# A sparse attention and Fourier mixing kernel: x added by GpSimd for six output items, a new item order, and U two items behind V

## The chip, the cores and the metric

The kernel runs on one core of a Trainium2 chip. The core has a matrix engine (TensorE, PE in the profile), a vector engine (VectorE, DVE), a scalar engine (ScalarE, ACT), GpSimd (POOL) and SyncE (SP), which work through their own instruction queues and wait for each other by semaphores. Matrix products land in PSUM, eight banks of 128 x 512 float32; everything else lies in SBUF. Sixteen DMA engines move data between SBUF and the device memory. The metric is the device time of one execution in microseconds; the median of three runs before the change is 427.61 us (427.32 to 427.89).

## The reference

The first half is causal attention on 8 batches and 8 heads, 576 positions, head size 64. Four heads see a local window of 32, four see the positions of the same residue modulo 32. Its output, x (8 x 576 x 512), goes through a Fourier mixing layer of 64 modes and a channel matrix:

```python
X = np.fft.rfft(x, axis=1)
Xr, Xi = (np.real(X[:, :n_modes]), np.imag(X[:, :n_modes]))
Yr = np.einsum('bmd,mde->bme', Xr, w_r) - np.einsum('bmd,mde->bme', Xi, w_i)
Yi = np.einsum('bmd,mde->bme', Xr, w_i) + np.einsum('bmd,mde->bme', Xi, w_r)
Y[:, :n_modes] = Yr + 1j * Yi
y = np.fft.irfft(Y, n=S, axis=1)
u = x + y
return (u + np.maximum(u @ w_ch, 0.0)).astype(np.float32)
```

So each output row is U + relu(V) with U = x + y and V = U @ w_ch. The output is 9.44 MB of float32.

## The kernel before

Three stages are interleaved by hand; the order of each engine's instructions is the order of the program text. The attention runs batch by batch. Beside it and after it the 64 modes' complex weights stream in (128 matrices' halves through GpSimd's DMA queue, 81 MB with the attention's inputs), and each mode is multiplied with the spectra of all 8 batches. In the meantime x @ w_ch and x itself are prepared in float16 (`v0s`, `xos`, and for the last 64 positions of each batch `v0h`, `xoh`), and as modes get ready, `renew` (L948) adds the contribution of three quarters of the modes to them. What is left for the end is the contribution of the last 16 modes.

The end, which the change is about, starts after the last mode (L1042). The output is cut into 18 items (L973 to L977). Items 0 to 15 are a pair of batches (2P, 2P+1) and one of four sets of 128 rows, t = 0 to 3; sets t and t+1 (t even) are the even and odd rows of the same 256. Items 16 and 17 are the last 64 rows of four batches each. The order before is, for P0 in (0, 2): t = 0 to 3 outside, P = P0, P0+1 inside, so neighbouring items are of different pairs of batches.

Every item k goes through these steps:

- `v_early(k)`, L984 to L987: two identity matmuls on TensorE copy the prepared x @ w_ch into a PSUM pair from pool `p` (three pairs of banks). `u_early(k)`, L989 to L992: two identity matmuls copy the prepared x into a PSUM pair, from pool `p` for even k and from pool `u` (one pair) for odd k.
- `new_rows`, L994 to L1003: for each batch of the item one matmul of 32 rows adds the last modes' part, from `zzs` to V and from `yys` to U. The 32 rows of batch b are those of the row group b modulo 4 of the TensorE array.
- `v_done(k)`, L1008 to L1013: ScalarE writes relu(V) to `rl` in SBUF, float32; four such tiles rotate.
- `u_done(k)`, L1015 to L1033: VectorE adds U from PSUM and `rl` to the output tile `osb` (five buffers, shared with the weights), and SP issues the output DMA, 512 KB. Item 0 goes in two halves. The last two items go as eight DMAs of 128 KB, from SP and ScalarE in turn.

After a prologue for items 0 and 1, the loop at L1065 runs U one item behind V: passes of V of k, passes of U of k-1, rows of V of k, rows of U of k-1, relu of k, addition and DMA of k-1. Before item 8 a held spectrum for batches 4 to 7 is made (L1066 to L1069), in a buffer of pool `p`. GpSimd does nothing in this stage; its last instruction is the last weight DMA (L190).

Of the kernel before, what the change touches and what calls it, by code (L numbers as in the profile page):

```python
# [12 lines left out]
AluOp = mybir.AluOpType  # L13
# [43 lines left out]
def kernel(  # L57
# [10 lines left out]
    nc = tc.nc  # L68
# [9 lines left out]
    def psum_pools(**bufs):  # L78
        pctx.close()
        pss.clear()  # L80
        for n, c in bufs.items():
            pss[n] = pctx.enter_context(
                tc.tile_pool(name="ps_" + n, bufs=c, space=PSUM)
            )

    def psum(kind, half=False, pair=False):
        if pair:
            return pss[kind].tile([128, 2, 512], FP, tag=kind, name=kind)
        if half:
            return pss[kind].tile([128, 1024], F16, tag=kind, name=kind)  # L90
        return pss[kind].tile([128, 512], FP, tag=kind, name=kind)
# [158 lines left out]
    def act_copy(out, in_):  # L250
        nc.scalar.activation(out=out, in_=in_, func=ACTF.Copy)  # L251
# [445 lines left out]
    def out_cols(t):  # L697
        if t < 4:
            return ds(256 * (t % 2) + 128 * (t // 2), 128)
        return ds(512, 64)  # L700

    v0s, xos = {}, {}
# [30 lines left out]
    def spec_z(g, bq, zp):  # L733
        for e in range(4):
            lhs = YS["YT"][:, e, g, ds(8 * bq, 8), :].rearrange("p x m -> p (x m)")
            nc.tensor.matmul(
                zp, lhs, w_chs["n"][:, e, :], start=(e == 0), stop=(e == 3)
            )
# [129 lines left out]
    xoh = [ptr.tile([128, DM], F16, name=f"xoh{i}") for i in range(4)]  # L868
    zzs = [ptr.tile([128, DM], F16, name=f"zz{i}") for i in range(B)]
    yys = [ptr.tile([128, DM], F16, name=f"yy{i}") for i in range(B)]  # L870
# [31 lines left out]
    A3 = cs["cFl"].rearrange("p a t m -> p (a t m)")[:, 0:S]  # L902
# [64 lines left out]
    for n, i in enumerate([3, 5, 7] + list(range(8, 21))):  # L967
        b, t = n // 2, n % 2 * 2
# [3 lines left out]

    items = []  # L973
    for P0 in (0, 2):
        items += [((2 * P, 2 * P + 1), t) for t in range(4) for P in (P0, P0 + 1)]
    items += [(range(b, b + 4), 4) for b in (0, 4)]
    LAST = len(items) - 1  # L977
    vps, ups, rls, osbs = {}, {}, {}, {}

    def own(item, kept, half):  # L980
        bs, t = item
        return [kept[b][:, t] for b in bs] if t < 4 else [half[b // 2] for b in bs[::2]]

    def v_early(k):  # L984
        vps[k] = psum("p", pair=True)
        for j, r in enumerate(own(items[k], v0s, v0h)):
            nc.tensor.matmul(vps[k][:, j], idn, r, start=True, stop=False)  # L987

    def u_early(k):  # L989
        ups[k] = psum(("p", "u")[k % 2], pair=True)  # L990
        for j, r in enumerate(own(items[k], xos, xoh)):
            nc.tensor.matmul(ups[k][:, j], idn, r, start=True, stop=False)  # L992

    def new_rows(k, acc, spectra):  # L994
        bs, t = items[k]
        for j, b in enumerate(bs):
            q = ds(32 * (b % 4), 32)
            o, cols = acc[:, j % 2], out_cols(t)
            if t == 4:
                o = acc[ds(64 * (b % 2), 64), j // 2]  # L1000
            nc.tensor.matmul(  # L1001
                o, A3[q, cols], spectra[b // 4][q], start=False, stop=True
            )  # L1003

    def pieces(k):
        return [slice(0, 1), slice(1, 2)] if k == 0 else [slice(0, 2)]

    def v_done(k):  # L1008
        rl = ptr.tile([128, 2, 576], FP, tag=("xT", "rl")[k // 2 % 2], bufs=2, name="rl")
        rls[k] = rl[:, :, 0:DM]  # L1010
        vp = vps.pop(k)
        for j in pieces(k):
            nc.scalar.activation(out=rls[k][:, j], in_=vp[:, j], func=ACTF.Relu)  # L1013

    def u_done(k):  # L1015
        bs, t = items[k]
        up, rl = ups.pop(k), rls.pop(k)
        osb = pw.tile([128, 2, DM], FP, tag="w", name="osb")
        for j in pieces(k):
            nc.vector.tensor_tensor(  # L1020
                out=osb[:, j], in0=up[:, j], in1=rl[:, j], op=AluOp.add
            )
            if t < 4:
                rows = out[:, ds(128 * (t - t % 2), 256), :].rearrange(
                    "b (p i) e -> p b i e", i=2
                )
                own_b = slice(bs[0] + j.start, bs[0] + j.stop)
                nc.sync.dma_start(rows[:, own_b, t % 2], osb[:, j])
        if t == 4:
            for b in bs:  # L1030
                (nc.scalar if b % 2 else nc.sync).dma_start(
                    out[b, ds(512, 64), :], osb[ds(64 * (b % 2), 64), b // 2 % 2, :]
                )  # L1033

    flush()
    rest = [(0, m) for m in range(SPLIT1, NM)] + [(1, m) for m in range(SPLIT0, NM)]
    late[22] = [lambda: v_early(0), lambda: v_early(1), lambda: u_early(0)]
    for i, (slot, m) in enumerate(rest):
        mode(slot, m)
# [16 lines left out]
    for k in range(2):  # L1056
        new_rows(k, vps[k], zzs)
    for k in range(2):
        v_done(k)
    for k in range(2):  # L1060
        if k:
            u_early(k)
        new_rows(k, ups[k], yys)
        u_done(k)
    for k in range(2, LAST + 2):  # L1065
        if k == 8:  # L1066
            held = psum("p", pair=True)[:, 0]
            spec_z(3, 1, held)
            act_copy(zzs[1], held)  # L1069
        if k <= LAST:  # L1070
            v_early(k)
        if k > 2:
            u_early(k - 1)
        if k <= LAST:
            new_rows(k, vps[k], zzs)
        if k > 2:
            new_rows(k - 1, ups[k - 1], yys)
        if k <= LAST:
            v_done(k)
        if k > 2:  # L1080
            u_done(k - 1)
    psum_pools()


# [28 lines left out]
```

## Time and profile before

| what | value |
|---|---|
| median of 3 runs | 427.61 us |
| profiled execution, span from first to last instruction | 426.7 us |
| TensorE busy | 346.4 us (81%), 4167 matmuls |
| VectorE / ScalarE / GpSimd busy | 234.7 / 218.3 / 110.7 us |
| DMA moved | 91.62 MB |
| V passes L987, U passes L992 | 36 matmuls each, 376 to 390 ns |
| relu L1013, 128x1024 | 17, median 1023 ns |
| addition L1020, 128x1024 | 17, median 1225 ns |
| output DMAs of 512 KB | 15, median 3.4 us from issue to landing |

A line of the timeline gives the start in us from the span's start, the time from the first start to the last end, the engine, the kernel's line, the operation, output and inputs, how many instructions are merged, and in brackets the idle time before and what ended it. Matmuls overlap in a pipeline, so two matmuls of 0.38 us can take 0.59 us together. In the slices of the span a digit is the busy share in tenths of one of forty equal slices (10.7 us each); in a table of windows each engine has its busy time and its count of instructions, and the last three columns are TensorE's granted clock, the mean busy share of the 16 DMA engines and the GB/s that they moved.

### The profile page before, as it was taken

The page shows a single profiled execution, that of the slowest core. Times are in us where ns is not written, and L with a number is a line of the kernel's source. Part 1 is how long each engine was busy: PE and PEld are TensorE (multiplying, and loading weights), DVE is VectorE, ACT ScalarE, POOL GpSimd, SP SyncE. Part 2 cuts the span into 40 slices and gives each one's busy share as a digit, 9 for nine tenths or more (in the row PEclk, how much of TensorE's full clock was granted, in tenths as well). Part 3 has the DMA queues.
Part 4 walks back from the last instruction along what each step waited for, and adds up shares of the span by engine and source line. Part 5 has one row for each costly group of instructions (what it writes and reads, how often), then busy time and mean ns, then how long its engine had stood idle before and what let it go on. Part 6 is the DMA issues. An engine that isn't in the chain of part 4 may idle for free.

```text
span 426.7 us, 9768 instructions
## 1 busy us (share of the span) xinstructions
PE 346.4 (81%) x4167; PEld 208.2 (49%) x4167; DVE 234.7 (55%) x466; ACT 218.3 (51%) x390; POOL 110.7 (26%) x196
## 2 busy tenths in 40 slices
PE   2977878769999698889768788878788867889993
PEld 2866767554656365566433344435444423445330
DVE  3788778851355154356113246746676354655884
ACT  1687678643656356556642235423442444443872
POOL 8332333322423222222222322222232222210000
PEclk9999899967999689999995889989999979989997
DMA  8999999999999999999999999999999999995698
GB/s 150 210 212 212 213 213 213 211 211 211 214 213 213 213 213 215 212 214 215 210 214 211 213 214 213 210 213 215 212 213 214 213 213 214 214 212 105 244 355 287
DMA packets 30938, 91.62 MB, mean 215 GB/s; under 512 B 4464, under 2 KB 5232, under 8 KB 30896
## 3 DMA queue, kind: packets, MB, share of 16 engines
q0 software_dynamic: 25168, 81.28, 96.2%
q1 hardware_dynamic: 4976, 9.13, 5.9%
q10 hardware_dynamic: 752, 0.61, 0.5%
q8 instruction: 32, 0.52, 0.5%
q14 instruction: 10, 0.08, 0.0%
HBM read 162.83 MB, written 9.44 MB: 404 GB/s over the span
## 4 chain that ended last, share of the span: by engine, by line
DMA 47%; PE 29%; DVE 14%; ACT 5%; issue 3%; DVEq 0%; POOL 0%; ACTq 0%; POOLq 0%
DMA wt<-in_moe_w_i_dram 38%; DMA wt<-in_moe_w_r_dram 7%; PE y L597 5%; DVE xb L241 3%; DVE kz L283 3%; PE p L987 2%; ACT X L251 2%; PE sc L532 2%; PE tp L413 2%; PE sc L459 1%; PE p L1001 1%; PE y L532 1%; PE p L760 1%; DVE yy L752 1%; DVE rec L240 1%
## 5 line engine op out<-in xcount | busy, mean ns | idle before, releaser
L597 PE MATMUL y<-wt,X 128*32 128x512 f16 (+1 forms) x448 | 70.9, 430 | 20.1 <-DMA wt<-in_moe_w_i_dram 20.1
L186 POOL DMA_DIRECT2D wt<-in_moe_w_r_dram x59 | 34.7, 588 | 126.4 <-PE y L597 56.3
L186 POOL DMA_DIRECT2D wt<-in_moe_w_i_dram x60 | 35.4, 590 | 68.3 <-DMA wt<-in_moe_w_i_dram 44.4
L597 PEld LDWEIGHTS <-X 128*32 128x32 f16 (+1 forms) x448 | 28.1, 140 | 39.4 <-DMA wt<-in_moe_w_i_dram 18.6
L727 DVE COPY xo<-tp 128x512 f16<-128x512 f16 x32 | 22.1, 691 | 36.8 <-PE tp L725 36.8
L726 ACT ACTIVATE v<-sc 128x512 f16<-128x512 f32 x32 | 19.1, 597 | 44.2 <-PE sc L717 44.2
L717 PE MATMUL sc<-w_cp,xT 128*128 128x512 f16 x128 | 36.9, 410 | 1.9 <-DVE xT L690 1.9
L489 ACT ACTIVATE PL<-sc 128x480 f16<-128x480 f32 (+1 forms) x48 | 27.0, 578 | 21.3 <-PE sc L475 21.0
L241 DVE TENSOR_TENSOR xb<-av,rec 90x256 f16<-90x256 f32 (+2 forms) x80 | 36.0, 450 | 2.8
L240 DVE RECIPROCAL rec<-av 90x4 f32<-90x4 f32 (+2 forms) x80 | 14.6, 183 | 39.3 <-PE av L504 28.2
L251 ACT ACTIVATE yr<-y 128x512 f16<-128x512 f32 x28 | 16.7, 597 | 36.8 <-PE y L597 35.6
L961 DVE TENSOR_TENSOR xo<-p,xo 128x1024 f16<-128x1024 f32 x16 | 19.6, 1225 | 21.7 <-PE p L760 21.7
L420 DVE COPY qT<-tp 128x576 f16<-128x576 f16 x16 | 11.9, 752 | 34.7 <-PE tp L413 34.7
L251 ACT ACTIVATE v<-p 128x1024 f16<-128x1024 f32 x16 | 16.4, 1023 | 23.1 <-PE p L760 23.1
L378 ACT ACTIVATE PL<-sc 90x360 f16<-90x360 f32 (+1 forms) x48 | 22.7, 490 | 7.0 <-PE sc L371 6.4
L251 ACT ACTIVATE v<-tp 128x640 f16<-128x640 f16 (+1 forms) x24 | 19.0, 807 | 11.8 <-PE tp L447 9.3
L413 PE MATMUL tp<-cI_s,ring 64*64 64x64 f16 x864 | 22.4, 197 | 2.7 <-DVE qT L420 2.4
L459 PE MATMUL sc<-cMl_s,cI_s 128*128 128x480 f16 (+1 forms) x48 | 19.4, 405 | 4.5 <-ACT PL L489 2.9
L276 PE MATMUL tp<-cI_s,ring 72*128 72x72 f16 x256 | 15.4, 207 | 8.7 <-DMA ring<-in_v_dram 7.1
L413 PEld LDWEIGHTS <-ring 64*64 64x64 f16 x864 | 17.5, 110 | 9.4 <-issue 5.4
L251 ACT ACTIVATE kz<-tp 64x360 f16<-64x360 f16 (+1 forms) x32 | 18.9, 592 | 6.2 <-PE tp L413 5.2
L1013 ACT ACTIVATE rl<-p 128x1024 f32<-128x1024 f32 (+1 forms) x19 | 18.4, 979 | 5.7 <-PE p L1001 3.1
(142 smaller groups left out, 737.9 us busy)
## 6 DMA issues: line engine op xcount, KB each, us to landing
wt<-in_moe_w_i_dram POOLq DMA_DIRECT2D x60, 512.0 KB, 18.8
wt<-in_moe_w_r_dram POOLq DMA_DIRECT2D x59, 512.0 KB, 17.7
out_dram<-osb SPq DMA_DIRECT2D x15, 512.0 KB, 3.4
ring<-in_v_dram POOLq DMA_DIRECT2D x8, 288.0 KB, 13.4
ring<-in_q_dram POOLq DMA_DIRECT2D x8, 288.0 KB, 13.6
ring<-in_k_dram POOLq DMA_DIRECT2D x8, 288.0 KB, 13.1
ring<-in_v_dram POOLq DMA_DIRECT2D x3, 512.0 KB, 14.8
ring<-in_q_dram POOLq DMA_DIRECT2D x3, 512.0 KB, 14.8
```

What stands on the lines that cost most here:

```text
L186: nc.gpsimd.dma_start(dst, rows)
L241: nc.vector.tensor_tensor(out=dst, in0=val.rearrange("p h (q c) -> p h c q", c=4), in1=rec[0:n, 0:pieces] .to_broadcast((n, pieces, 64)) . ...
L251: nc.scalar.activation(out=out, in_=in_, func=ACTF.Copy)
L378: nc.scalar.activation(out=PS[0:n, ds(POFF[t], 4 * n)], in_=scp[0:n, 0 : 4 * n], func=ACTF.Exp, scale=SCALE,)
L413: nc.tensor.transpose(tp[ds(64 * hp, 64), ds(64 * i, 64)], qn[ds(64 * hp, 64), ds(64 * (9 * g + i), 64)], idn[ds(64 * hp, 64), ds(64 * hp, ...
L459: nc.tensor.matmul(scp[:, 0 : n * times].rearrange("p (h x) -> p h x", h=times), idn, mask_rows("cMl", n, times), start=True, stop=False,)
L489: nc.scalar.activation(out=dst, in_=src, func=ACTF.Exp, scale=SCALE)
L597: nc.tensor.matmul(yp[ds(a, 32), :], Xh[half][pr, c].rearrange("p b r (h m) -> p (b r h) m", h=2)[:, :, mm % 32], wt[pr, XC[c], :], start= ...
L717: nc.tensor.matmul(vp, xT[:, ch], w_chs["cp"][:, ch, :], start=(ch == 0), stop=(ch == 3),)
L726: nc.scalar.activation(out=v0, in_=vp, func=ACTF.Copy)
L727: nc.vector.tensor_copy(out=xo.rearrange("p (h q c) -> p h q c", h=2, c=4), in_=tp[:, 0:512].rearrange("p (h c q) -> p h q c", h=2, c=4),)
L961: nc.vector.tensor_tensor(out=xo, in0=up[:, 0:n], in1=xo, op=AluOp.add)
```

## The change

Three things change together. First, the item order: for each half, t = (0, 1) of P0, then of P0+1, then t = (2, 3) of both, so that neighbouring items are the even and the odd rows of the same batches, and items k and k-2 are of different pairs of batches. Second, `LAG = 2`: U of item k-2 goes with V of item k, also in the prologue, where U of items 0 and 1 was written out ahead of the loop. Third, for items 4, 6, 8, 10, 12 and 14 (`X_LATE`) the identity passes of x are left out, the rows of y start the accumulation (`fresh`), and GpSimd adds x onto the relu in `rl`, in place, one 128x512 addition for each of the two batches. GpSimd also gets an instruction ahead of them that reloads its function library.

```diff
     for P0 in (0, 2):
-        items += [((2 * P, 2 * P + 1), t) for t in range(4) for P in (P0, P0 + 1)]
+        items += [
+            ((2 * P, 2 * P + 1), t + i)
+            for t in (0, 2)
+            for P in (P0, P0 + 1)
+            for i in range(2)
+        ]
...
+    LAG = 2
+    X_LATE = range(4, 16, 2)
...
     def u_early(k):
         ups[k] = psum(("p", "u")[k % 2], pair=True)
+        if k in X_LATE:
+            return
...
-    def new_rows(k, acc, spectra):
+    def new_rows(k, acc, spectra, fresh=False):
...
-                o, A3[q, cols], spectra[b // 4][q], start=False, stop=True
+                o, A3[q, cols], spectra[b // 4][q], start=fresh, stop=True
...
             nc.scalar.activation(out=rls[k][:, j], in_=vp[:, j], func=ACTF.Relu)
+        if k in X_LATE:
+            for j, r in enumerate(own(items[k], xos, xoh)):
+                nc.gpsimd.tensor_tensor(
+                    out=rls[k][:, j], in0=rls[k][:, j], in1=r, op=AluOp.add
+                )
...
-    for k in range(2):
-        if k:
-            u_early(k)
-        new_rows(k, ups[k], yys)
-        u_done(k)
-    for k in range(2, LAST + 2):
+    for k in range(LAST + 1 + LAG):
+        u = k - LAG
         if k == 8:
...
-        if k <= LAST:
+        if 2 <= k <= LAST:
             v_early(k)
-        if k > 2:
-            u_early(k - 1)
-        if k <= LAST:
+        if u > 0:
+            u_early(u)
+        if 2 <= k <= LAST:
             new_rows(k, vps[k], zzs)
-        if k > 2:
-            new_rows(k - 1, ups[k - 1], yys)
-        if k <= LAST:
+        if u >= 0:
+            new_rows(u, ups[u], yys, u in X_LATE)
+        if 2 <= k <= LAST:
             v_done(k)
-        if k > 2:
-            u_done(k - 1)
+        if u >= 0:
+            u_done(u)
```

## The prediction

> **What bounds the kernel now.** I read the span's forty slices first, then the end of the timeline, then one-microsecond windows, because the change touches only the last stage (the output items, from 395 us on).
>
> ```profile
> PE   2977878769999698889768788878788867889993
> DMA  8999999999999999999999999999999999995698
> GB/s 150 210 212 212 213 213 213 211 211 211 214 213 213 213 213 215 212 214 215 210 214 211 213 214 213 210 213 215 212 213 214 213 213 214 214 212 105 244 355 287
> ```
>
> Up to slice 36 the weights fill the DMA engines. In the last four slices TensorE and the DMA engines are both nearly full, so either may be the limit. The timeline at the stage's start (start us, duration us, engine, line, operation):
>
> ```profile
> 395.10 0.40 PE L1001 MATMUL p<-zz,cFl_s 32*128 32x512 f16 x4 [0.29 <-ACT zz L251]
> 395.33 0.39 PE L1001 MATMUL p<-yy,cFl_s 32*128 32x512 f16 x2
> 395.53 3.11 ACT L1013 ACTIVATE rl<-p 128x512 f32<-128x512 f32 x4 [0.48 <-PE p L1001]
> 396.16 1.29 DVE L1020 TENSOR_TENSOR osb<-p,rl 128x512 f32<-128x512 f32 x2 [0.55 <-ACT rl L1013]
> 396.67 0.59 PE L987 MATMUL p<-v,cI_s 128*128 128x512 f16 x2
> 396.88 22.13 SPq L1028 DMA_DIRECT2D out_dram<-osb  x17
> 397.19 0.39 PE L1001 MATMUL p<-zz,cFl_s 32*128 32x512 f16 x2
> 397.56 1.23 DVE L1020 TENSOR_TENSOR osb<-u,rl 128x1024 f32<-128x1024 f32 x1
> ```
>
> Item 0 has its y rows at 395.33, its first addition at 396.16 and its first output DMA at 396.88; the identity passes of V of item 2 (L987) start only at 396.67, when the relu of item 0 has emptied their PSUM buffer. One steady item:
>
> ```profile
> 410.40 0.61 PE L987 MATMUL p<-v,cI_s 128*128 128x512 f16 x2
> 410.85 0.59 PE L992 MATMUL u<-xo,cI_s 128*128 128x512 f16 x2
> 411.38 0.39 PE L1001 MATMUL p<-zz,cFl_s 32*128 32x512 f16 x2
> 411.38 0.39 PE L1001 MATMUL u<-yy,cFl_s 32*128 32x512 f16 x2
> 411.81 1.02 ACT L1013 ACTIVATE rl<-p 128x1024 f32<-128x1024 f32 x1 [0.27 <-PE u L1001]
> 411.90 1.23 DVE L1020 TENSOR_TENSOR osb<-u,rl 128x1024 f32<-128x1024 f32 x1
> ```
>
> From here come the intervals: V passes to U passes 0.45 (0.43 at most places), U passes to rows 0.53, rows to the next V passes 0.32; 1.30 us an item, TensorE full. The four row matmuls run side by side. The relu starts 0.43 after the rows, VectorE's addition 0.53 after them. ScalarE (1.02) and VectorE (1.23, or 1.14 to 1.16 back to back) have room. Now the windows; the last two columns are DMA share and GB/s:
>
> ```profile
> 398.00:399.00 1.00, 1.00 (x8) 0.31 (x7) 0.79 (x1) 0.67 (x2) 0.00 (x0) 1.00 1.03 381
> 399.00:400.00 1.00, 1.00 (x8) 0.29 (x6) 0.93 (x1) 0.99 (x1) 0.00 (x0) 1.00 0.47 164
> 400.00:408.00 8.00, 7.86 (x49) 2.55 (x46) 6.42 (x6) 5.75 (x7) 0.00 (x0) 1.00 1.00 373
> 408.00:409.00 1.00, 1.00 (x8) 0.30 (x6) 0.98 (x1) 0.94 (x1) 0.00 (x0) 1.00 0.31 115
> 409.00:421.00 12.00, 10.69 (x72) 3.23 (x68) 10.89 (x10) 8.19 (x8) 0.00 (x0) 1.00 1.02 380
> ```
>
> This decides it. Although the chain of waits names TensorE, the DMA engines are at 1.00 to 1.02 with 373 to 380 GB/s. An item is 512 KB (524,288 B), so it costs the DMA 1.38 us, more than TensorE's 1.30. The DMA idles only at 399 (0.5 us, before item 1 arrives), 0.1 us near 401, and at 408 (0.69 us). The last hole comes from the held spectrum at item 8 (L1068), after which VectorE's additions go from 404.25 to 406.72. So the stage is about as long as its DMA work plus the wait for its first item.
>
> **The change, part by part.** *Removed:* twelve identity passes of x, two for each of items 4, 6, ... 14. A pair is 0.43 us, together 2.58 us of TensorE, on the path that the profile draws, but under a DMA that needs 1.38 an item anyway. Worth nothing once the DMA has a backlog; what hides it is the output stream itself. Were that cover gone, all 2.58 us would count.
>
> *Moved: U by two items instead of one.* The y rows of item 0 now stand in TensorE's queue behind the V passes and z rows of item 2, and these wait for item 0's whole relu. So the y rows run with item 2's z rows at 397.19 instead of 395.33, and the first addition starts at 397.19 + 0.53 = 397.72 instead of 396.16. The same for item 1: V passes of item 3 at 397.6 (after relu 1, as before), U passes 398.05, rows 398.6, addition 399.13 instead of 397.56: 1.57 us later. Everything behind it on VectorE and on SP's queue shifts by that. The addition ends 1.23 later, SP issues 0.03 after that, and data flows 0.88 after the issue (396.88 to the 397.76 at which the 0.24 share of the window 397 to 398 begins), so item 1 flows from 401.27, not from 399.70. Between item 0 and 1 the DMA starves as before.
>
> *Moved: the item order.* Items k and k-2 are now of different pairs of batches, as k and k-1 were, so the four row matmuls still run beside each other: nothing. If they didn't, 0.2 us an item of TensorE time, under the DMA too. The z rows of items 0 and 1 now share row groups (at most 0.2 us, hidden by the relu wait). Output DMAs keep count, size and 2 KB rows; neighbouring rows are written one item apart instead of two. No row prices that; I bound it by the spread of full one-microsecond windows, 365 to 393 GB/s about 380: 0.9 us either way over 25 us, and take nothing.
>
> *Added: twelve GpSimd additions, 128x512.* The nearest rows of this trace:
>
> ```profile
> L329 POOL COPY PL<-cT_s 128x576 f16<-128x576 f16 x1 | 1.2, 1161 | 0.0
> L1097 POOL MEMSET const-float32-0.0<- 128x1 f32 x1 | 0.1, 98 | 0.2 <-issue 0.2
> ```
>
> That is (1161 - 98)/575 = 1.85 ns an element with one input. Low end, if the second input is free: 0.10 + 512 x 1.85 ns = 1.04 us; high end, if the inputs are read in turn: 1.99 us. I take the copy's own 1.16 (it is strided, the addition is not), 2.32 us an item. The Trainium skill (GPSIMD Engine Reference, Performance versus the Vector engine) advises against elementwise work there and gives 4497 ns for a 2048-element two-input addition; by that estimate the pair would be 2.25 us and the sum 0.1 us smaller.
>
> Every second item takes one pair and the DMA needs 2 x 1.38 = 2.76 us for two items, so GpSimd keeps up; what it costs is latency. Item 4: V passes at 399.05 (they take the PSUM buffer that item 0's addition frees), U passes of item 2 399.48, rows 400.0, relu 400.45 to 401.47, GpSimd to 401.53 + 2.32 = 403.85. VectorE was free at 403.0, after additions of items 2 and 3 at 400.55 and 401.84, so it waits 0.9 us, and behind it on its queue wait item 5, their DMAs on SP, and the V passes of item 8, which take item 4's buffer. DMA: item 2 flows from 402.69, item 3 ends at 405.45, item 4 can flow only from 403.91 + 1.23 + 0.03 + 0.88 = 406.05: a hole of 0.60. At item 8 the same steps give 0.29 (relu to 407.27, GpSimd to 409.65, data from 411.85 against 411.56). At item 14 the backlog covers it (data ready 419.7, DMA busy to 420.1). The hole at the held spectrum (0.69) closes, as items 6 and 7 come late and 1.3 us apart. One more instruction on GpSimd, a reload of its function library ahead of the additions, I cost at nothing: the last weight DMA is issued there at 382.31 + 0.52, the first addition is wanted at 401.53, so 18.7 us cover it, and beyond that each microsecond costs one. The same page (GPSIMD Engine Reference, Instruction dispatch) puts a first call after a load at about 6 us; no row here shows one.
>
> *The tail.* The last two items' 1.05 MB took from 421.3 to 424.75, 3.45 us, against 2.76 at 380 GB/s, as the last DMAs were issued at 422.3, a microsecond after item 15 was through. With a longer backlog they are issued some 0.4 us after it, so up to 0.6 may come off; I take 0.2.
>
> **Sum:** 1.57 (start) + 0.60 + 0.29 + 0.05 (holes behind GpSimd, and one before item 2) - 0.69 - 0.10 (old holes) - 0.2 (tail) = +1.5 us. On this execution's span 426.7 that is 428.2; the median 427.61 lies 0.9 above the span, so **429.1 us**.
>
> **Rivals.** *The backlog absorbs everything but the start.* With GpSimd at 1.04 and deeper buffers the holes vanish and the tail runs at the full rate: 1.57 - 0.79 - 0.69 = +0.1, so 427.7; half of that recovered gives 428.4. For it: VectorE and ScalarE have room. Against: the PSUM ring of three buffers, of which U holds one longer. Place: the DMA windows from 401 to 421.
>
> *TensorE was the bound after all (faster).* If an item's DMA can take under 1.30 us, for instance because neighbouring rows come together, TensorE sets the end: -2.58, plus one more item of lag, 1.30: -1.3, so 426.3. For it: the chain of waits runs through L987 and L992 throughout. Against: twelve full microseconds at 1.02. It decides once a full window shows over 524 KB/1.30 us = 403 GB/s; the highest here is 393.
>
> *GpSimd becomes the bound (much slower).* Above 1.38 us an addition the pairs queue up. At 1.99: item 14 is ready at 401.53 + 6 x 3.97 = 425.4, three more additions of 1.16 and the last to 430.1, where it ended at 421.28 before: +8.8, so 436.4. At 1.45 it is about 430.5.
>
> **Chances.** Forecast (428.5 to 430.5) 0.62; backlog absorbs 0.18; TensorE was the bound 0.08; GpSimd bound 0.12. A measurement of this kernel tells 0.2%, 0.86 us, from no change: slower is the first and last, 0.74, within it 0.18, faster 0.08. The range is 427.6 to 430.6: it takes in the absorbed case and a GpSimd addition up to about 1.45 us, and leaves out the fast and the very slow.
>
> **What would show it.** First output DMA at 398.4 instead of 396.88; then DMA windows near 1.0 except at items 1, 4 and 8; VectorE's waits on GpSimd at the even items; TensorE with idle time that it did not have, waiting for PSUM; GpSimd additions of 1.0 to 1.3 us. A first DMA before 397.5, full windows above 400 GB/s, or additions above 1.4 us would make the prediction wrong.

## The result, and the profile after

The median is 429.14 us (428.73 to 430.33, 8 runs) against 427.81 us (427.32 to 428.57, 8 runs) for the kernel before, measured beside it. The ratio is 1.0032, interval 1.0021 to 1.0043: slower by 1.3 us, more than the 0.2% that the measurement can tell from no change. The profiled execution took 429.28 us, and its span is 427.5 us.

The forty slices of the span, after (tenths busy, then GB/s):

```profile
PE   2979788759998698889669678876888858988892
POOL 7333332322423222222221322232222222210480
DMA  8999999999999999999999999999999999994598
GB/s 149 211 212 214 214 212 213 211 211 211 215 213 212 213 214 212 215 214 213 211 214 212 213 213 213 206 212 214 214 213 213 212 214 214 214 212 94 214 373 298
```

Up to the 36th slice little differs. In the last slices GpSimd now has a 4 and an 8 where it did nothing before, TensorE is less full, and the output comes later: 94 and 214 GB/s in the 37th and 38th slices, where it was 105 and 244.

The timeline after, at the start of the last stage (start, duration, engine, line, operation):

```profile
394.80 0.61 PE L1010 MATMUL p<-zz,cFl_s 32*128 32x512 f16 x4 [0.29 <-ACT zz L251]
395.23 3.11 ACT L1022 ACTIVATE rl<-p 128x512 f32<-128x512 f32 x4 [0.48 <-PE p L1010]
396.37 0.59 PE L994 MATMUL p<-v,cI_s 128*128 128x512 f16 x2 [0.96 <-ACT rl L1022]
396.89 0.39 PE L1010 MATMUL p<-zz,cFl_s 32*128 32x512 f16 x2
396.90 0.39 PE L1010 MATMUL p<-yy,cFl_s 32*128 32x512 f16 x2
397.42 1.29 DVE L1034 TENSOR_TENSOR osb<-p,rl 128x512 f32<-128x512 f32 x2 [2.11 <-PE p L1010]
398.14 0.94 SPq L1042 DMA_DIRECT2D out_dram<-osb  x2
398.77 1.23 DVE L1034 TENSOR_TENSOR osb<-u,rl 128x1024 f32<-128x1024 f32 x1
```

The first rows run at 394.80 (395.10 before). TensorE then waits 0.96 us for the relu of item 0 before it can do the V passes of item 2, and the y rows of item 0 stand behind these: 396.90. VectorE waits 2.11 us for them. The first output DMA is issued 3.34 us after the first rows, where it was 1.78 (396.88 - 395.10).

The waits on GpSimd, from the timeline after:

```profile
401.14 4.50 POOL L1025 TENSOR_TENSOR rl<-rl,xo 128x512 f32<-128x512 f32 x4 [18.37 <-ACT rl L1022]
403.44 1.22 DVE L1034 TENSOR_TENSOR osb<-p,rl 128x1024 f32<-128x1024 f32 x1 [0.85 <-POOL rl L1025]
409.18 1.22 DVE L1034 TENSOR_TENSOR osb<-p,rl 128x1024 f32<-128x1024 f32 x1 [0.78 <-POOL rl L1025]
411.59 0.59 PE L1001 MATMUL u<-xo,cI_s 128*128 128x512 f16 x2 [0.20 <-DVE osb L1034]
416.87 1.23 DVE L1034 TENSOR_TENSOR osb<-p,rl 128x1024 f32<-128x1024 f32 x1 [0.54 <-POOL rl L1025]
```

VectorE waits for GpSimd at items 4, 8 and 14, 2.2 us in all, and TensorE now waits for VectorE (0.20 at 411.59). The windows after (start:end, length, busy time and count of PE, PEld, DVE, ACT and POOL, then clock, DMA share and GB/s):

```profile
399.00:402.00 3.00, 3.00 (x21) 0.82 (x19) 2.86 (x3) 2.45 (x3) 0.86 (x1) 1.00 0.83 308
402.00:403.00 1.00, 0.76 (x8) 0.38 (x4) 0.59 (x1) 1.00 (x2) 1.00 (x2) 1.00 0.45 168
403.00:411.00 8.00, 7.56 (x45) 2.32 (x44) 6.59 (x6) 6.20 (x8) 6.77 (x7) 1.00 1.02 381
411.00:412.00 1.00, 0.80 (x4) 0.19 (x2) 1.00 (x2) 0.52 (x1) 0.78 (x2) 1.00 0.86 315
412.00:421.00 9.00, 7.35 (x49) 2.16 (x48) 8.43 (x8) 4.90 (x5) 4.14 (x4) 1.00 1.03 378
```

The DMA engines idle for 0.5 us between items 0 and 1 (0.17 of three microseconds), for 0.55 us in 402 to 403 and 0.14 us in 411 to 412, and are full otherwise. TensorE does 7.35 us of work in the last nine, where 12 microseconds of before had 10.69. The hole at the held spectrum is gone. From the first rows to the last output data, the stage took 29.65 us before (395.10 to 424.75) and 31.08 us after (394.80 to 425.88): 1.43 us longer, close to the 1.33 us between the medians. These ends take the share of the last microsecond as if it had been moved at the full rate; the very last data move until 425.05 and 426.05, which makes it 1.30 us.

### The profile page after: what moved, and what is told of

Its sections match the earlier page's. It is cut to its first block, busy times and chain, and to the rows that moved or that the text cites. A ratio compares the mean times of both kernels' runs of the same rounds, so it can differ in the third digit from the quotient of the medians.

```text
span 427.5 us, 9764 instructions
## 1 busy us (share of the span) xinstructions
PE 338.4 (79%) x4155; PEld 205.5 (48%) x4155; DVE 234.4 (55%) x466; ACT 217.7 (51%) x390; POOL 124.3 (29%) x208
## 4 chain that ended last, share of the span: by engine, by line
DMA 52%; PE 16%; DVE 5%; ACT 2%; issue 2%; POOL 1%; DVEq 0%; ACTq 0%; POOLq 0%
DMA wt<-in_moe_w_i_dram 41%; DMA wt<-in_moe_w_r_dram 7%; PE y L597 4%; DMA ring<-in_v_dram 4%; PE sc L717 3%; DVE yy L752 1%; DVE osb L1034 1%; POOL rl L1025 1%; ACT rl L1022 1%; PE p L994 1%; PE p L1010 1%; PE tp L725 1%; ACT X L251 1%; PE y L532 1%; PE u L1001 1%
## 5 line engine op out<-in xcount | busy, mean ns | idle before, releaser
L597 PE MATMUL y<-wt,X 128*32 128x512 f16 (+1 forms) x448 | 68.2, 416 | 24.5 <-DMA wt<-in_moe_w_i_dram 24.2
L717 PE MATMUL sc<-w_cp,xT 128*128 128x512 f16 x128 | 35.5, 398 | 1.9 <-DVE xT L690 1.9
L532 PEld LDWEIGHTS <-xb 108*128 108x128 f16 (+2 forms) x176 | 15.5, 106 | 11.2 <-DVE xb L241 7.1
## 6 DMA issues: line engine op xcount, KB each, us to landing
wt<-in_moe_w_i_dram POOLq DMA_DIRECT2D x60, 512.0 KB, 18.3
```

The source lines that it names most:

```text
L532: nc.tensor.matmul(xp[:, ds(192 * cp, 192)].rearrange("p (f m) -> p f m", f=3), xb[b][0:n, base + t, ds(128 * cp, 128)], F[0:n, :, t, :], ...
L597: nc.tensor.matmul(yp[ds(a, 32), :], Xh[half][pr, c].rearrange("p b r (h m) -> p (b r h) m", h=2)[:, :, mm % 32], wt[pr, XC[c], :], start= ...
L717: nc.tensor.matmul(vp, xT[:, ch], w_chs["cp"][:, ch, :], start=(ch == 0), stop=(ch == 3),)
```

## The experiments

The theory: the output stream ends the kernel, so the deeper lag costs its late start, GpSimd adds holes, and the relief of TensorE is worth little. The rivals were those of the prediction. Medians stand beside that of the kernel before in the same set of runs: 427.87 us for the first four, 427.86 for those with half the output and for i1 and i2, 428.02 for j1, j2 and the first run of the old order. Each ratio has its 95% interval.

### The lag and the order, without GpSimd (to the kernel after)

```diff
     LAG = 2
-    X_LATE = range(4, 16, 2)
+    X_LATE = ()
```

> The changed order and U two items behind V, but no GpSimd additions: all items get their identity passes of x again. Theory (the output DMA stream is the limit and the change starts it 1.5 us late): the late start stays, the waits for GpSimd go, so 428.5 to 429.1 against 427.8 before and 429.1 after, although TensorE has 2.58 us more to do than after. Rival 1 (GpSimd's additions are the cost): 427.8 or less. Rival 2 (TensorE sets the end): 429.1 + 2.6 = 431.7.

Measured: 428.61 us, ratio 1.0018 (1.0009 to 1.0027). Windows of this run:

```profile
398.00:399.00 1.00, 1.00 (x12) 0.34 (x8) 0.94 (x2) 0.90 (x1) 0.00 (x0) 1.00 0.56 207
407.00:408.00 1.00, 1.00 (x9) 0.26 (x7) 1.00 (x1) 0.77 (x1) 0.00 (x0) 1.00 0.61 227
408.00:421.00 13.00, 11.55 (x75) 3.54 (x72) 11.79 (x11) 8.19 (x8) 0.00 (x0) 1.00 1.02 380
```

The first output DMA is issued 3.33 us after the first rows (397.57 after 394.24), as in the kernel after. The hole at the held spectrum (407) is still there, at 0.39 us instead of 0.69, and then the stream is full to 421. So the lag with the new order makes the kernel slower, by 0.74 us, with no work on GpSimd: the late start of 1.56 us, less what the smaller holes give back (0.88 us in all from 399 on, where the kernel before has 1.3). No run has the new order with a lag of one, so a share of the order in this is not ruled out by measurement.

### The kernel before without the x passes

```diff
         ups[k] = psum(("p", "u")[k % 2], pair=True)
+        if k in range(4, 16, 2):
+            return
...
-            new_rows(k - 1, ups[k - 1], yys)
+            new_rows(k - 1, ups[k - 1], yys, k - 1 in range(4, 16, 2))
```

> The kernel before, but for items 4, 6, ... 14 the identity passes of x are left out and nothing takes their place (x is missing in these items). Theory: TensorE does 2.58 us less, but only the DMA holes near 401 and at 408 close (0.1 + 0.69), so 427.0 to 427.3. Rival 2 (TensorE sets the end): 427.8 - 2.6 = 425.2.

Measured: 427.31 us, ratio 0.9988 (0.9979 to 0.9997), 0.01 above the expected range. Its stage took 29.15 us (394.08 to 423.23), 0.5 less than before. Its first rows come 1.02 us earlier than in the profile of before, so the microsecond that shows the held spectrum is now 407 to 408:

```profile
407.00:408.00 1.00, 1.00 (x11) 0.24 (x10) 0.90 (x2) 0.48 (x2) 0.00 (x0) 1.00 0.82 303
```

The DMA share is 0.82 where before had 0.31: TensorE is ahead by then, and the hole is 0.18 us instead of 0.69. So 2.58 us of TensorE work are worth 0.56 us here, mostly that hole.

### The kernel after without GpSimd's additions

```diff
-        if k in X_LATE:
-            for j, r in enumerate(own(items[k], xos, xoh)):
-                nc.gpsimd.tensor_tensor(
-                    out=rls[k][:, j], in0=rls[k][:, j], in1=r, op=AluOp.add
-                )
```

> The changed kernel without the twelve GpSimd additions (x is missing in these items). Theory: VectorE's waits for GpSimd (0.85, 0.78 and 0.54 us) go, but only the small DMA holes behind them close, the late start stays: 428.4 to 428.9. Rival 1 (GpSimd's additions are the cost): 427.8 or less. Rival 2: as after, 429.1, since TensorE's work is the same.

Measured: 428.55 us, ratio 1.0022 (1.0011 to 1.0032). Against the run with the lag alone (428.61) it has 2.58 us less TensorE work and the same time: with the lag in place, this work is worth nothing that can be measured. Against the kernel after (1.0032), the waits on GpSimd are worth about 0.4 to 0.6 us (by the ratios and by the medians).

### The kernel after with items 0 and 1 as early as before

```diff
-    for k in range(LAST + 1 + LAG):
+    for u in range(2):
+        if u:
+            u_early(u)
+        new_rows(u, ups[u], yys)
+        u_done(u)
+    for k in range(2, LAST + 1 + LAG):
         u = k - LAG
```

(With it, the loop's three conditions on `u` become `u > 1`.)

> The changed kernel, but U of items 0 and 1 is written out ahead of the loop as before, and U runs two items behind from item 2 on. Theory: the first output DMA is back 1.2 us earlier than after, but between items 1 and 2 the DMA now waits about 1 us, as V of items 2, 3 and 4 go first; what is left is that item 2 and all behind it come some 0.6 us earlier than after: 428.3 to 428.8. Rival (the start doesn't matter, the waits for GpSimd do): 429.1.

Measured: 428.48 us, ratio 1.0019 (1.0010 to 1.0028). Windows and two additions of this run's timeline:

```profile
400.00:401.00 1.00, 1.00 (x8) 0.21 (x6) 0.93 (x2) 0.73 (x2) 0.50 (x1) 1.00 0.64 227
401.00:402.00 1.00, 0.76 (x7) 0.38 (x7) 0.95 (x1) 1.00 (x2) 1.00 (x2) 1.00 0.47 178
402.00:404.00 2.00, 2.00 (x12) 0.62 (x11) 1.19 (x2) 1.48 (x2) 2.00 (x3) 1.00 1.02 381
404.00:405.00 1.00, 0.91 (x7) 0.28 (x5) 1.00 (x2) 0.65 (x2) 1.00 (x1) 1.00 0.38 141
405.00:410.00 5.00, 4.65 (x32) 1.41 (x28) 4.03 (x5) 4.07 (x5) 3.77 (x5) 1.00 1.01 378
```

```profile
399.43 1.22 DVE L1034 TENSOR_TENSOR osb<-p,rl 128x1024 f32<-128x1024 f32 x1 [1.14 <-PE p L1010]
402.81 1.22 DVE L1034 TENSOR_TENSOR osb<-p,rl 128x1024 f32<-128x1024 f32 x1 [0.86 <-POOL rl L1025]
```

The early start buys only 0.56 to 0.66 us of 1.57 back (by the ratios and by the medians). The lag is merely taken up one step later: item 2's addition waits 1.14 us for its rows, and the stream has 0.89 us of hole in 400 to 402. At 404 it has 0.62 us, behind the 0.86 us that VectorE waits for GpSimd at item 4. This is the hole of 0.60 that the prediction worked out.

### Half the output, with and without the x passes

Each item sends one batch of its two; the second kernel adds the edit of the x passes from above.

```diff
                 own_b = slice(bs[0] + j.start, bs[0] + j.stop)
-                nc.sync.dma_start(rows[:, own_b, t % 2], osb[:, j])
+                own_b = slice(bs[0] + j.start, bs[0] + j.start + 1)
+                if j.start == 0:
+                    nc.sync.dma_start(rows[:, own_b, t % 2], osb[:, 0:1])
         if t == 4:
-            for b in bs:
+            for b in bs[::2]:
```

> The kernel before with half of the output written: each item's DMA carries one of its two batches, and of the last two items the even batches alone (the odd batches' rows are missing). Theory: the engines then set the end; the last addition stays where it was, 26.2 us after the stage's first rows, and its DMAs land about 1.2 us sooner, so 426.4 to 427.0 against 427.8. Rival 2 (TensorE sets the end anyway): 427.8 less at most 0.5 for the shorter last transfers.

> Half of the output written, and for items 4, 6, ... 14 the identity passes of x left out as well (odd batches' rows and x in these items are missing). Theory: with the DMA out of the way leaving out the passes is worth more than the 0.5 us that it gave with the whole output; VectorE, 1.14 to 1.23 an addition, is the next limit, its last addition was 1.1 us earlier, so 425.2 to 425.8, 1.0 to 1.3 below the half output alone. Rival 2: 2.6 below the half output alone, 424.0.

Measured: 426.90 us, ratio 0.9975 (0.9964 to 0.9985), and without the x passes 425.62 us, ratio 0.9944 (0.9932 to 0.9956), where the window 398 to 418 has a DMA share of only 0.51 (a window of the second kernel):

```profile
398.00:418.00 20.00, 18.30 (x120) 5.76 (x116) 17.58 (x15) 15.32 (x16) 0.00 (x0) 1.00 0.51 193
```

Less TensorE work alone gives 0.56 us, half the output alone 0.96, both together 2.24: more than the sum of 1.52. The last addition starts 24.96 us after the first rows in the kernel before and with half the output, and 23.91 us after them in both kernels without the x passes: the stream doesn't hold the engines up, but with the whole output it ends too late to let their 1.05 us through. In the kernel before, the stream and the engines' pace end nearly together, and relief of one runs into the other soon.

### Closing the holes of the kernel before: halves

Items are added and sent in halves, so that data reaches the DMA earlier and VectorE's additions don't pile up around the held spectrum. Four variants of one line; the second also does the two 64-row items earlier.

```diff
-        for j in pieces(k):
+        for j in [slice(0, 1), slice(1, 2)] if t < 4 else [slice(0, 2)]:
```

> The kernel before, but for items 0 to 15 VectorE adds, and SP sends, each of the two batches on its own (256 KB DMAs); nothing else changes, TensorE's work neither. Theory: the first half of every item reaches the DMA 0.6 us sooner, so the holes before item 1 (0.55), near 401 (0.1) and at 408 (0.69) mostly close: 426.5 to 427.1 against 427.8. Rival 2 (TensorE sets the end): 427.8 or, as VectorE has 0.07 us more an item, 428 to 429.

```diff
-    items += [(range(b, b + 4), 4) for b in (0, 4)]
+    items.insert(8, (range(0, 4), 4))
+    items.insert(15, (range(4, 8), 4))
...
-                (nc.scalar if b % 2 else nc.sync).dma_start(
+                (nc.gpsimd if b % 2 else nc.sync).dma_start(
...
-        if k == 8:
+        if k == 9:
```

> As the one before, and the two items of 64 rows (eight DMAs of 64 partitions) go as items 8 and 15 and not last, their odd batches' DMAs issued by GpSimd, so that the span ends with two whole items. Theory: the slow tail (1.05 MB in 3.45 us, where 380 GB/s would take 2.76) is mixed with other transfers; 0.3 to 0.6 less than with the halves alone: 426.0 to 426.8. Rival (64-partition transfers are slow wherever they stand): the same as the halves alone.

```diff
-        for j in pieces(k):
+        for j in [slice(0, 1), slice(1, 2)] if k in (0, 7, 8, 9) else [slice(0, 2)]:
```

> The kernel before, but items 7, 8 and 9, the ones behind the held spectrum, are added and sent in halves like item 0. Theory: the hole of the DMA at 408 (0.69) closes to 0.1 and about 0.5 of it reaches the end: 427.2 to 427.6 against 427.8. Rival (halves cost the DMA or SP more than they give, as the run with halves everywhere may suggest): 427.8 to 428.5.

```diff
-        for j in pieces(k):
+        for j in [slice(0, 1), slice(1, 2)] if k in (0, 1, 7, 8, 9) else [slice(0, 2)]:
```

> As the one before, and item 1 in halves too, against the hole of 0.55 before it. Theory: 426.8 to 427.3. Rival (the slow issue of the fourth output DMA, 1.59 us with halves everywhere where it is 0.38 before, comes from the close spacing of the first four): it comes again here and the time is 427.8 to 428.8.

Measured, in this order: 428.93 us, ratio 1.0020 (1.0011 to 1.0030); 429.55, 1.0036 (1.0024 to 1.0048); 428.01, 1.0004 (0.9994 to 1.0013); 428.25, 1.0004 (0.9992 to 1.0016). All four missed the ranges of the theory, and none beats the kernel before; the first, third and fourth lie in the ranges of their rivals. In the first, the fourth output DMA took long to issue on SP's queue:

```profile
397.85 1.59 SPq L1028 DMA_DIRECT2D out_dram<-osb  x1
```

Where before it took 0.38 us, it took 1.59 us, and the DMA share from 398.75 to 399.90 was 0.09. The third (items 0, 7, 8 and 9) closes the hole at the held spectrum, but its own fourth issue, 0.85 us, opens one of 0.59 us in 400 to 401, where the kernel before had 0.10 near 401:

```profile
399.50 0.85 SPq L1028 DMA_DIRECT2D out_dram<-osb  x1
```

```profile
400.00:401.00 1.00, 1.00 (x8) 0.31 (x7) 0.93 (x2) 0.73 (x2) 0.00 (x0) 1.00 0.41 154
401.00:420.00 19.00, 17.73 (x112) 5.47 (x109) 16.63 (x17) 13.59 (x14) 0.00 (x0) 1.00 1.02 380
420.00:421.00 1.00, 0.00 (x0) 0.00 (x0) 0.46 (x1) 0.00 (x0) 0.00 (x0) 1.00 0.73 197
```

From 401 on the stream is full, and nothing is gained: it runs dry at 420 instead. Since it has to wait for the engines there, the hole at 400 doesn't set its end. The addition of item 16 starts 23.81 us after the first rows (418.10 after 394.29), as in the kernel before (23.82); TensorE's work is the same. So a hole closed in the middle comes back at the end, unless the engines are faster too.

### The kernel after with the item order of before

```diff
-        items += [
-            ((2 * P, 2 * P + 1), t + i)
-            for t in (0, 2)
-            for P in (P0, P0 + 1)
-            for i in range(2)
-        ]
+        items += [((2 * P, 2 * P + 1), t) for t in range(4) for P in (P0, P0 + 1)]
```

> The changed kernel with the item order of before (t outside, the pairs of batches inside), so that items k and k-2 are of the same pair and their row matmuls share row groups of the array. Theory: TensorE pays 0.2 us more an item, on average 1.3 instead of 1.08, still under the DMA's 1.38; at the start it adds 0.2 to 0.4 to the late first item: 429.1 to 429.7. Rival 2 (TensorE sets the end): 16 x 0.2 = 3.2 more than after, 432.3.

Measured: 431.20 us (429.49 to 431.99), ratio 1.0067 (1.0046 to 1.0088): 1.5 us above what was expected. In its profiled execution TensorE ran at half its clock early in the stage (the third column from the right is the clock):

```profile
395.90:396.90 1.00, 0.97 (x6) 0.21 (x5) 0.00 (x0) 0.91 (x2) 0.00 (x0) 1.00 0.00 0
396.90:400.40 3.50, 3.50 (x12) 0.84 (x11) 1.75 (x3) 1.95 (x2) 0.00 (x0) 0.51 0.40 146
400.40:402.00 1.60, 1.60 (x10) 0.43 (x9) 1.05 (x2) 0.63 (x2) 0.00 (x0) 1.00 0.06 19
```

The same kernel once more:

> The run with the item order of before once more, for a second profile: in the first TensorE's granted clock was 0.51 from 396.9 to 400.4, and the times spread from 429.5 to 432.0. If the row groups alone cost the 2 us, this profile has the full clock throughout and a time near 431; if the clock did, a profile with the full clock has a time near 429.5 and its first additions at after's distances.

Measured: 430.04 us, a single run, beside 427.39 for the kernel before, at the full clock in this stage. Its timeline at the start:

```profile
396.47 0.39 PE L1005 MATMUL p<-zz,cFl_s 32*128 32x512 f16 x2
396.70 0.38 PE L1005 MATMUL p<-yy,cFl_s 32*128 32x512 f16 x2
398.68 1.23 DVE L1029 TENSOR_TENSOR osb<-u,rl 128x1024 f32<-128x1024 f32 x1 [0.22 <-issue]
399.93 1.02 SPq L1037 DMA_DIRECT2D out_dram<-osb  x1
400.19 1.22 DVE L1029 TENSOR_TENSOR osb<-p,rl 128x1024 f32<-128x1024 f32 x1 [0.28 <-PE p L1005]
```

And two of its windows:

```profile
408.00:409.00 1.00, 1.00 (x7) 0.17 (x6) 0.96 (x1) 0.95 (x2) 1.00 (x2) 1.00 0.63 234
411.00:412.00 1.00, 1.00 (x7) 0.31 (x7) 1.00 (x1) 0.95 (x2) 1.00 (x2) 1.00 0.77 291
```

The z rows of item k and the y rows of item k-2 are now of the same batches, so of the same row groups, and they run one pair after the other (0.23 us apart) instead of side by side. The additions of the first items come every 1.5 us instead of every 1.3, longer than the 1.38 us that the stream takes for an item. The DMA share from 400 to 402 is 0.36, because the issue of item 1's DMA took 1.02 us here, where it took 0.39 in the first execution and in the kernel after. That moves a hole more than it adds one: item 1 flowed from 399.93 + 1.02 + 0.5 = 401.45, items 1 to 3 took 4.14, to 405.59, and item 4's data, issued at 404.64, was ready only at 405.52.

Neither of the two outcomes that were set out beforehand came: the time lies between them, and the additions are not at the distances of the kernel after. At full clock the old order with a lag of two is about 0.9 us slower (430.04 against 429.14; by the kernel before beside each it is 2.65 - 1.33 = 1.3), in one execution. The halved clock fits the rest between the two profiled executions: with it the addition of item 2 starts 7.36 us after the first rows, without it 5.80, and the times are 431.32 and 430.04. For the other five times (429.49 to 431.99) no profile shows the clock in this stage.

## Why the prediction was right, and where it was not

*The bound.* It held: after the first items the stream runs at 1.01 to 1.03 and 378 to 381 GB/s, and no full window shows more than 393 GB/s, where TensorE would have been the bound from 403. (In the last four of the forty slices, though, TensorE has 9993 and the DMA engines 5698 tenths, so they are not both nearly full there; the windows, not the slices, carry this reading.) But "worth nothing" for the removed x passes holds only with the lag (428.61 against 428.55). In the kernel before they are worth 0.56 us, and the doubled relief shows that the engines end close behind the stream. The prediction's sum wasn't hurt, since it had booked that part as the closed hole at the held spectrum.

*The start, +1.57.* Right in mechanism and size: the first output DMA comes 1.56 us later relative to the first rows (3.34 against 1.78) and the addition of item 1 1.51 us later (3.97 against 2.46). Two runs bear it out: the lag with the new order is slower without any work on GpSimd, and an early start wins back only 0.6 us, as most of the lag of two is paid one item later.

*The holes, +0.60, +0.29 and +0.05.* The wait at item 4 was predicted as 0.9 us and is 0.85; GpSimd's additions took 1.15 to 1.16 us each, as taken from the copy's row. The hole is not where it was predicted, though. In the profile of after, the DMA idles 0.55 us at 402 to 403, before item 2, because the issue of item 2's DMA took 1.02 us:

```profile
401.32 1.02 SPq L1042 DMA_DIRECT2D out_dram<-osb  x1
```

That made items 2 and 3 late enough for item 4 to come in time. Item 2's data could flow from 401.32 + 1.02 + 0.5 = 402.84, items 2 and 3 took 2.76, to 405.60, and item 4's data was ready at 403.44 + 1.22 + 0.03 + 0.88 = 405.57. With an issue of 0.38 they would have been through some 0.6 us earlier, and the hole would have stood at item 4, as it does in the run with the early start (0.62). One of the two had to come; the sum is the same. At item 8 the hole is 0.14, not 0.29.

*The old holes, -0.69 and -0.10.* Both closed. That alone was worth nothing in the kernel before (the third of the runs with halves: 428.01 against 428.02), because there the stream then waits for TensorE at the end; here it can count, since TensorE has less to do, as in the kernel before without the x passes.

*The tail, -0.2.* Not there: the last 1.05 MB took about 3.5 us (422.35 to 425.88), as before. The windows of the tail, after:

```profile
422.00:423.00 1.00, 0.00 (x0) 0.00 (x0) 0.00 (x0) 0.00 (x0) 0.00 (x0) 1.00 1.03 311
423.00:424.00 1.00, 0.00 (x0) 0.00 (x0) 0.00 (x0) 0.00 (x0) 0.00 (x0) 1.00 1.03 342
424.00:425.00 1.00, 0.00 (x0) 0.00 (x0) 0.00 (x0) 0.00 (x0) 0.00 (x0) 0.57 0.91 299
```

The prediction took the tail's excess over 380 GB/s for idle time that a longer backlog would fill. The engines are busy in it, at 1.03, and move only 311 and 342 GB/s: it is mostly the rate of the 64-row transfers, and a backlog doesn't change that. The second run with halves agrees: there the second of the two items of 64 rows has whole items behind it, and the window 421 to 422 shows 254 GB/s at a DMA share of 1.00, and 423 to 424, with whole items, 393 GB/s at 1.03.

*The sum.* Holes of before, 0.53 + 0.10 + 0.69 = 1.3 us; of after, 0.5 + 0.55 + 0.14 = 1.2. So 1.56 - 0.1 = 1.46 us was to be expected from the parts as they came, and the stage became 1.43 us longer (1.30 by the very last data). The predicted +1.5 is made of a start that was exact, holes that cost 0.25 us too much, and a tail that gave 0.2 us too much. That the last two cancel is luck, and so is part of the hit of 429.1 by 429.14: the difference of the medians is 1.33, not 1.5, and the kernel before ran 0.2 us slower beside it (427.81) than the 427.61 that the prediction built on. By the runs, the 1.33 us are 0.74 for the lag with the new order, nothing that can be measured for the x passes, and 0.4 to 0.6 for the waits on GpSimd.

*From span to median.* This step was wrong, and it cancelled. The span came out at 427.5, not 428.2; the median lies 1.6 above it, not 0.9. In the profiled executions of the experiments the time exceeded the span by 1.74 to 1.84 us (1.78 in that of after), so by its span the profiled execution of before took some 428.5 us itself and was a long one for its kernel. The time of 429.1 rests on the difference of +1.5, which both executions carry alike.

*The item order at nothing.* That the new order keeps the four row matmuls side by side is right. The aside, that without it 0.2 us an item would lie under the DMA, is refuted: without the new order the kernel after was about 0.9 us slower even at full clock (one execution). Against the profile of after, its first output DMA comes 0.16 us later after the first rows (3.50 against 3.34), the holes up to 402 are 0.22 us larger (1.28 against 1.06) and those at 408 and 411 are 0.46 us larger (0.60 against 0.14): 0.84 in all. With additions 1.5 us apart the stream gathers too little backlog, at the start and also for the pauses at the held spectrum and at item 8's wait for GpSimd.

*The library reload at nothing.* Two configuration rows of 42 ns at 382.8 on GpSimd's queue, and its first addition starts at 401.14, released by the relu: hidden under 18.3 us. What it takes without such cover no run shows. The order in which rows reach memory was taken at nothing too; the full windows before and after (380, and 378 to 381 GB/s) show no difference.

*What stays open.* Why one of the first output DMAs takes longer to issue in some executions, and what sets off the halved clock (both below): both are only observed, never varied by themselves.

## What to carry to other kernels

Before relieving an engine, find out per stage what the stage would end with then: here 2.58 us of TensorE work bought 0.56 us by itself, and nothing behind the output stream once the lag was paid. A deeper lag in an in-order queue delays the first item by more than an item's time (1.5 us here, against 1.30), and where a saturated output stream follows, that delay is the main price of the change; taking the lag up one item later won back only 0.6 us. Until such a stream has a backlog, delays reach the end: with the old order, 0.2 us an item on TensorE cost about 0.4 us at the start and 0.5 us at two later pauses of the additions.

## What the hardware showed unexpectedly

The issue of the fourth output DMA on SP's queue took 0.38 us in the kernel before, in the runs with the lag and the new order alone, without x passes, without additions and with the early start, but 1.02 in the kernel after, and 1.59, 1.94, 0.85 and 1.69 us in the four kernels with halves, in the order above. In the second execution with the old order it was the third, item 1's, with 1.02 us, where the first execution took 0.39. Each time the DMA share behind it fell to 0.09 or less for a quarter of a microsecond or longer. So it comes and goes between executions of one program. The distances of the first four issues alone don't set it off: they are 0.60, 1.28 and 1.30 us both in the kernel after (1.02) and in the run with the lag and the new order alone (0.38).

TensorE's clock fell to 0.51 for 3.5 us in the kernel after with the old order, after TensorE had waited 1.17 us for the relu of item 0, and stayed at 1.00 in a second execution of the same program with the same wait of 1.17 us. The Trainium skill (TensorE: Matmul & The Clock Gate, Part 1: The HAM clock gate) tells of a free-running window of 3413 ns and of a halved clock after at least one idle window. The length of 3.5 us agrees with that window, while a wait of 1.17 us is short of it; in the 3.5 us before the drop (393.40 to 396.90) TensorE was busy for 2.05.

The output DMAs of 64 partitions move fewer bytes in the same busy time: 311 and 342 GB/s at a DMA share of 1.03 in the tail after, where those of 128 partitions hold 378 to 381. These DMAs are also smaller (128 KB); the DMAs of 256 KB from 128 partitions in the kernels with halves show no such loss (375 to 391 GB/s at 1.01 to 1.05 in the microseconds from 400 to 419 of the first), so size down to 256 KB is not the reason, but 128 KB from 128 partitions was not run.
